# Attention, router and experts on one core: expert weights loaded in four parts, and row loads queued behind stores

## The chip, the cores and the metric

The kernel runs on one core of one Trainium2 chip. The metric is the device time of one launch in microseconds, the median of several runs without a profile. The profile is one further execution of the same program, and it is somewhat longer. A core has TensorE (PE in the profile; its weight loads are PEld), VectorE (DVE), ScalarE (ACT), GpSimd (POOL) and SyncE (SP). The last two also issue the DMA transfers here, and all transfers share 16 DMA engines.

## The reference

Block-causal attention with 8 batches, 8 heads, 576 positions and head size 64 gives 4608 rows of 512. A noisy router picks two of eight experts for each row, and an expert is two matrix products with a relu between them.

```python
scores = scale * np.matmul(q, k.transpose(0, 1, 3, 2))
mask = block_i >= block_j                    # blocks of 64 positions
attn = softmax(np.where(mask, scores, -1e9))
x = np.matmul(attn, v)                       # then as rows (4608, 512)
# ...
noisy_logits = x @ w_gate + np.log1p(np.exp(x @ w_noise)) * noise
top2 = np.argpartition(-noisy_logits, 2, axis=1)[:, :2]
top2_w = softmax of the two chosen logits
for e in range(8):                           # w1[e]: (512, 1024), w2[e]: (1024, 512)
    for k in range(2):
        mask = top2[:, k] == e
        h = np.maximum(x[mask] @ w1[e], 0.0)
        out[mask] += top2_w[mask, k, None] * (h @ w2[e])
```

## The kernel before

Attention goes through four groups of two batches, in 26 score slots each (`UG` = 26, `NG` = 4, so slots 0 to 103). A dictionary `at(slot, ...)` hangs other work on the slots: transposes, products with v, router steps, and scatters. A scatter writes 128 rows, sorted by expert, to an area `xd` in HBM; there are two halves of the rows, each with its own `xd` and `yd`.

The expert stage then works on 16 tiles. A tile is one expert and one half, 640 rows; the order is experts 0 to 3 of half 0, experts 0 to 3 of half 1, then experts 4 to 7 with both halves in turn. Layer 1 of a tile has 8 steps of 8 matmuls, layer 2 has 5 steps of 8. Step 0 of the next tile's layer 1 stands ahead of the layer 2 of this tile. Slots are counted on through these steps.

```python
def load_w(pool, e):                         # f32 in HBM, bf16 in SBUF: 1 MB each there
    w1sb = pool.tile([P, DB, F], BF16, tag="w1")
    nc.gpsimd.dma_start(out=w1sb, in_=moe_w1[e].rearrange("(b p) f -> p b f", p=P))
    w2sb = pool.tile([P, FB, Dm], BF16, tag="w2")
    nc.gpsimd.dma_start(out=w2sb, in_=moe_w2[e].rearrange("(b p) d -> p b d", p=P))
    wload[e] = (w1sb, w2sb)

def load_x(b):                               # rows of tile b, transposed on the way
    xg = ffn["x"].tile([P, DB, CAP], BF16, tag="xg", name="xg")      # 3 buffers
    ins = nc.sync.dma_start_transpose(out=xg, in_=xd[half][e * CAP:(e + 1) * CAP, 0:Dm])
    # ... waits for all scatters of the half

def layer1(b, fb):
    hp = sc_ps.tile([P, 2, 512], F32, tag="sc")                      # 2 buffers
    # ... 8 matmuls of 320 columns: hp <- w1sb, xg
    ins = nc.scalar.activation(out=hs[b][:, fb, :]..., in_=hp[:, :, 0:NW], func=AF.Relu)
    pace.append(ins.ins.name)

def layer2(b, c):
    yp = av_ps.tile([P, Dm], F32, tag="av")                          # 2 buffers
    # ... 8 matmuls of 512 columns: yp <- hs, w2sb
    if e + 1 < E:
        ysb = ffn["y"].tile([P, Dm], BF16, tag="ysb", bufs=4)
        nc.scalar.activation(out=ysb, in_=yp, func=AF.Copy, scale=w)
        nc.sync.dma_start(out=yd[half][...], in_=ysb)
    if c < LT[e]:                                                    # LT = 0,1,2,3,3,4,5,5
        yo = ffn["y"].tile([P, Dm], F32, tag="yo", bufs=4)
        nc.vector.scalar_tensor_tensor(out=yo, in0=yp, scalar=w, in1=ygs.pop((b, c)), ...)
        ins = nc.gpsimd.indirect_dma_start(out=out, ..., in_=yo)     # finished rows

def gather(b, c):                            # the rows' results of their other expert
    yg = ffn["y"].tile([P, Dm], BF16, tag="yg", bufs=GB, name="yg")  # 6 buffers
    ins = nc.gpsimd.indirect_dma_start(out=yg, ..., in_=yd[half][0:e * CAP, :], ...)
    tc.add_manual_dep(ins.ins, pace[-2], ...)

GJ = (2, 3, 4, 6, 7)                         # steps of layer 1 at which gathers go out
# ...
at(2 * UG + 24, load_w, wE, 0)
at(3 * UG + 15, load_w, wE, 1)
for u in range(NG * UG):
    score_unit(*divmod(u, UG))
    run(u)
    if u == 3 * UG + 18:
        # ... pools for rows and for expert 2
        load_x(0); load_rec(0); load_x(1); load_x(2); load_w(wM, 2)
# ...
for fn, b, j in steps:
    fn(b, j)
    if fn is layer1:
        if j == 0 and b and b + 2 < NB and b + 2 != 4:
            load_x(b + 2)
        if (b, j) == (3, 4):
            load_rec(1)
            load_x(4)
        if (b, j) in WL:
            load_w(*WL[b, j])
        if j in GJ and GJ.index(j) < LT[SEQ[b][1]]:
            gather(b, GJ.index(j))
    run(slot)
    slot += 1
    if slot == NG * UG + 6:
        # ... pools
        load_w(wL, 3)
        WL = {(5, 7): (wE, 4), (7, 3): (wE, 5), (9, 3): (wM, 6), (11, 3): (wL, 7)}
```

Every engine takes its instructions in the order of the program. A scatter or a gather waits for a recent activation (`pace[-2]`), which spreads these over time. Weights have no such wait; they wait for their buffers alone.

Of the kernel before, what the change touches and what calls it, by code (L numbers as in the profile page):

```python
# [9 lines left out]
BF16 = mybir.dt.bfloat16  # L10
# [9 lines left out]
def kernel(  # L20
# [12 lines left out]
    nc = tc.nc  # L33

    B, H, S, D = q.shape
    N, Dm = out.shape
    E = moe_w_gate.shape[1]
    F = moe_w1.shape[2]
    assert Dm == H * D and N == B * S
    P = 128  # L40
    DB = Dm // P
    FB = F // P
# [21 lines left out]
    UG = 2 * UN  # L64
# [32 lines left out]
    wE = main.enter_context(tc.tile_pool(name="wE", bufs=2))  # L97
# [109 lines left out]

    wload = {}

    def load_w(pool, e):  # L210
        w1sb = pool.tile([P, DB, F], BF16, tag="w1")
        nc.gpsimd.dma_start(out=w1sb, in_=moe_w1[e].rearrange("(b p) f -> p b f", p=P))
        w2sb = pool.tile([P, FB, Dm], BF16, tag="w2")
        nc.gpsimd.dma_start(out=w2sb, in_=moe_w2[e].rearrange("(b p) d -> p b d", p=P))
        wload[e] = (w1sb, w2sb)


    def transpose_qk(g, nm, ch):
# [256 lines left out]
    def load_x(b):  # L475
        half, e = SEQ[b]
        xg = ffn["x"].tile([P, DB, CAP], BF16, tag="xg", name="xg")
        ins = nc.sync.dma_start_transpose(out=xg, in_=xd[half][e * CAP:(e + 1) * CAP, 0:Dm])
        for nm in scat[half]:
            tc.add_manual_dep(ins.ins, nm, SYNC_DEP, reason="rows landed")  # L480
        xgs[b] = xg

    def load_rec(half):
        rc = rec_pool.tile([P, E, CT, NREC], I32, tag="rc", name="rc")
        ins = nc.sync.dma_start(out=rc.rearrange("p e c w -> p (e c) w"),
                                in_=xd[half].bitcast(I32)[0:OVB, Dm // 2:Dm // 2 + NREC]
                                .rearrange("(c p) w -> p c w", p=P))
        for nm in scat[half]:
            tc.add_manual_dep(ins.ins, nm, SYNC_DEP, reason="rows landed")
        rs[("rc", half)] = rc  # L490
# [76 lines left out]
    def gather(b, c):  # L567

        half, e = SEQ[b]
        yg = ffn["y"].tile([P, Dm], BF16, tag="yg", bufs=GB, name="yg")  # L570
        if len(gathers) < GB:
            nc.gpsimd.memset(yg, 0.0)
        gathers.append(b)
        ins = nc.gpsimd.indirect_dma_start(  # L574
            out=yg, out_offset=None, in_=yd[half][0:e * CAP, :],
            in_offset=bass.IndirectOffsetOnAxis(ap=orows[half][:, e, c:c + 1], axis=0),
            bounds_check=e * CAP - 1, oob_is_err=False)
        tc.add_manual_dep(ins.ins, pace[-2], SYNC_DEP, reason="spreads the descriptors over time")
        ygs[(b, c)] = yg
# [8 lines left out]
    NB = len(SEQ)  # L588
# [3 lines left out]
    def at(slot, fn, *args):  # L592
        todo.setdefault(slot, []).append((fn, args))

    def run(slot):
        for fn, args in todo.pop(slot, ()):
            fn(*args)
# [96 lines left out]
            at(r0 + r1 + j, scatter, g, j)  # L694
    at(8, clear_x, 0, 7)
    at(UG + 8, clear_x, 1, UG + 7)
    at(2 * UG + 24, load_w, wE, 0)
    at(3 * UG + 15, load_w, wE, 1)
    for u in range(NG * UG):
        score_unit(*divmod(u, UG))  # L700
        run(u)
        if u == 3 * UG + 18:
            raws_up.close()
            ffn["x"] = raws_up.enter_context(tc.tile_pool(name="xgp", bufs=3, side="right", reuse_waits="tile"))
            wM = raws_up.enter_context(tc.tile_pool(name="wM", bufs=1, side="right", reuse_waits="tile"))
            load_x(0)
            load_rec(0)
            load_x(1)
            load_x(2)
            load_w(wM, 2)  # L710

    slot = NG * UG
    at(slot + 6, read_rec, 0)
# [8 lines left out]
    for i in range(2):  # L722
        run(slot)
        slot += 1
    WL = {}
    for fn, b, j in steps:
        fn(b, j)
        if fn is layer1:
            if j == 0 and b and b + 2 < NB and b + 2 != 4:
                load_x(b + 2)  # L730
            if (b, j) == (3, 4):
                load_rec(1)
                load_x(4)
            if (b, j) == (4, 3):
                read_rec(1)
# [7 lines that stand above are left out]
            top.close()  # L743
            wL = top.enter_context(tc.tile_pool(name="wL", bufs=1, reuse_waits="tile"))
            ffn["y"] = top.enter_context(tc.tile_pool(name="yp", bufs=4, reuse_waits="tile"))
            load_w(wL, 3)
            WL = {(5, 7): (wE, 4), (7, 3): (wE, 5), (9, 3): (wM, 6), (11, 3): (wL, 7)}
    assert not todo, sorted(todo)
    sched.__exit__(None, None, None)

# [5 lines left out]
    with tc.If(rs["over"] > 0):  # L756
# [4 lines left out]
        for g in range(NG):  # L761
# [5 lines left out]
            for idx in range(TG):  # L767
                for p0, tok in token_blocks(g, idx):
                    nc.sync.dma_start(out=token_order(tok_w[tok:tok + 64, :]), in_=wd[p0:p0 + 64, g, idx, :])
                    nc.sync.dma_start(out=token_order(tok_s[tok:tok + 64, :]),  # L770
                                      in_=slots[p0:p0 + 64, g * TG + idx, 0:1])
        for half in range(NH):
            with tc.For_i(half * TH * P, (half + 1) * TH * P, P) as r0:
# [6 lines left out]
                    out=xo.bitcast(I32), out_offset=None, in_=xd[half].bitcast(I32),  # L780
# [9 lines left out]
                for e in range(E):  # L790
                    load_w(fb_w, e)
                    w1sb, w2sb = wload[e]
# [44 lines left out]
```

The softmax here doesn't subtract the row's maximum and nothing guards it: scores larger than these inputs give would overflow.

## Time and profile before

| | |
|---|---|
| Time, median of 3 runs | 541.73 us (540.43 to 545.04) |
| Span of the profiled execution | 564.4 us |
| Mean granted TensorE clock | 0.856 |
| DMA | 79.76 MB moved, 141 GB/s mean; 101365 of 140949 packets under 512 B |
| Weight loads | 16 of 1 MB, issued by GpSimd, 0.84 us (w1) and 0.96 us (w2) of GpSimd each |
| Transposing row loads | 16, issued by SyncE, 2.3 to 18.2 us of SyncE each, median 5.2 |
| Scatters, gathers, stores of finished rows | 72, 46 and 46, about 1 us of GpSimd each |

The page gives the busy time of each engine and its share of the span, then the span in 40 slices of 14.1 us: a digit is the busy share of a slice in tenths, and PEclk is the clock that TensorE was granted, in tenths of full speed. A row of the groups has the line of the kernel, engine, operation, what is written and read, the shapes and the count, then the busy time and the mean length of one, then the idle time just before them and who ended it. A timeline has start and length in us; the brackets hold the idle time before it and its releaser. Instructions of the same kind that follow each other are one row with a count. In the chain of waits each row is a piece of the chain that ended last: start, length, what it was. A GpSimd row that issues a DMA shows the time of issuing alone; where the chain names a DMA, the row runs from its issue to its landing.

### The profile page before, as it was taken

Reading aid. Unit: us, or ns where it says so; the run is one execution under the profiler, and the core shown is the slowest. Engines: PE = TensorE matmul, PEld = TensorE weight load, DVE = VectorE, ACT = ScalarE, POOL = GpSimd, SP = SyncE. Lnnn points to the kernel's source line nnn. Section 1 sums busy time; section 2 is a strip of 40 time slices with the busy share of each in tenths; the row PEclk is TensorE's granted clock in tenths of the full one; section 3 lists DMA queues with packets and bytes.
Section 4 is the critical chain, followed back from the end, with each engine's and each line's share of the span. In section 5 each row is a group of like instructions: output and inputs, shape, how many; then the busy total and the mean of one; then the engine's idle time right before and its main releaser. Section 6 shows DMA issues by size and latency. Waiting matters only on the chain.

```text
span 564.4 us, 9944 instructions
## 1 busy us (share of the span) xinstructions
PE 446.0 (79%) x3944; PEld 268.1 (48%) x3944; DVE 175.5 (31%) x490; ACT 238.9 (42%) x319; POOL 247.2 (44%) x291
## 2 busy tenths in 40 slices
PE   3796976796778668786969996977986995999980
PEld 2464654464345445444535553543553562555540
DVE  4474795388348627200103000100100201112220
ACT  1856754454446313333425442442451451554210
POOL 9683454583744416375322021142242452556550
PEclk9857976778676569998979997997997997999995
DMA  9999998295946999832582496496597588634230
GB/s 137 135 166 229 96 212 175 80 102 99 154 143 120 188 204 195 205 130 84 148 123 80 94 157 123 120 156 154 156 157 175 146 159 210 136 120 146 104 105 27
DMA packets 140949, 79.76 MB, mean 141 GB/s; under 512 B 101365, under 2 KB 130807, under 8 KB 140896
## 3 DMA queue, kind: packets, MB, share of 16 engines
q0 software_dynamic: 70304, 55.78, 59.6%
q1 hardware_dynamic: 70592, 23.27, 20.4%
q8 instruction: 33, 0.54, 0.4%
q14 instruction: 20, 0.16, 0.1%
HBM read 68.28 MB, written 34.21 MB: 182 GB/s over the span
## 4 chain that ended last, share of the span: by engine, by line
PE 46%; DMA 17%; issue 14%; POOL 9%; DVE 7%; ACT 3%; another core or an unknown queue 1%; POOLq 0%; SPq 0%; DVEq 0%; ACTq 0%
PE hp L533 16%; PE yp L545 15%; DMA xg<-xd 6%; PE sc L276 4%; POOL yg L574 4%; POOL out_dram L556 3%; PE av L313 3%; PE tp L238 2%; DMA yg<-yd,orow 2%; PE av L324 2%; DMA t<-in_q_dram 2%; PE tp L342 2%; DMA t<-in_k_dram 2%; DMA vt<-in_v_dram 2%; DMA out_dram<-yo,trow 1%
## 5 line engine op out<-in xcount | busy, mean ns | idle before, releaser
L533 PE MATMUL hp<-xg,w1sb 128*128 128x320 bf16 x1024 | 150.8, 308 | 26.6 <-ACT hq L536 15.0
L545 PE MATMUL yp<-w2sb,hq 128*128 128x512 bf16 x640 | 150.5, 393 | 25.5 <-DVE yo L554 21.5
L533 PEld LDWEIGHTS <-w1sb 128*128 128x128 bf16 x1024 | 102.6, 101 | 72.5 <-issue 23.2
L279 ACT ACTIVATE esc<-sc 128x1024 bf16<-128x1024 f32 x96 | 95.1, 1028 | 85.6 <-PE sc L276 53.9
L536 ACT ACTIVATE hq<-hp 128x640 bf16<-128x640 f32 x128 | 89.6, 704 | 88.7 <-PE hp L533 81.1
L554 DVE SCALAR_TENSOR_TENSOR yo<-yp,wrow,yg 128x512 f32<-128x512 f32 x46 | 34.3, 750 | 283.5 <-ACT ysb L550 200.1
L545 PEld LDWEIGHTS <-hq 128*128 128x128 bf16 x640 | 64.0, 100 | 106.6 <-issue 37.9
L459 POOL DMA_INDIRECT xd<-xr,slots x72 | 71.6, 995 | 79.6 <-issue 34.4
L550 ACT ACTIVATE ysb<-yp,wrow 128x512 bf16<-128x512 f32 x70 | 48.1, 687 | 121.4 <-PE yp L545 97.7
L556 POOL DMA_INDIRECT out_dram<-yo,trow x46 | 45.8, 996 | 110.7 <-DVE yo L554 107.3
L574 POOL DMA_INDIRECT yg<-yd,orow x46 | 47.2, 1027 | 81.9 <-ACT hq L536 54.5
L276 PE MATMUL sc<-hq 64*128 64x512 bf16 (+4 forms) x320 | 48.4, 372 | 11.5 <-ACT esc L279 9.9
L313 PE MATMUL av<-vt,esc 128*128 128x65 bf16 x640 | 38.8, 221 | 7.8 <-DVE xr L328 6.1
L313 PEld LDWEIGHTS <-esc 128*128 128x128 bf16 x640 | 30.5, 114 | 23.7 <-DVE xr L328 10.6
L205 POOL DMA_DIRECT2D vt<-in_v_dram x40 | 33.8, 876 | 14.7 <-PE av L324 10.6
L238 PE MATMUL tp<-ident,t 128*64 128x128 bf16 x512 | 29.4, 285 | 7.2 <-DVE hq L243 3.9
L328 DVE TENSOR_TENSOR xr<-av,rden 128x256 bf16<-128x256 f32 x72 | 30.6, 424 | 2.5
L238 PEld LDWEIGHTS <-t 128*64 128x64 bf16 x512 | 23.3, 149 | 15.8 <-DMA t<-in_q_dram 7.2
L245 DVE COPY hq<-tp 128x1024 bf16<-128x1024 bf16 (+1 forms) x24 | 25.0, 1042 | 6.3 <-PE tp L238 3.7
L327 DVE RECIPROCAL rden<-av 128x4 f32<-128x4 f32 x72 | 12.6, 174 | 43.6 <-PE av L313 15.2
L324 PE MATMUL av<-vt,esc 128*64 128x65 bf16 (+1 forms) x320 | 17.2, 226 | 10.9 <-issue 6.3
L276 PEld LDWEIGHTS <-hq 64*128 64x128 bf16 x320 | 12.5, 100 | 21.7 <-issue 14.4
(118 smaller groups left out, 213.8 us busy)
## 6 DMA issues: line engine op xcount, KB each, us to landing
yd<-ysb SPq DMA_DIRECT2D x70, 128.0 KB
w1sb<-in_moe_w_dram POOLq DMA_DIRECT2D x8, 1024.0 KB
w2sb<-in_moe_w_dram POOLq DMA_DIRECT2D x8, 1024.0 KB
t<-in_q_dram POOLq DMA_DIRECT2D x16, 256.0 KB
t<-in_k_dram POOLq DMA_DIRECT2D x16, 256.0 KB
vt<-in_v_dram POOLq DMA_DIRECT2D x32, 128.0 KB
xd<-zero SPq DMA_DIRECT2D x32, 99.0 KB
nz_all<-in_moe_noise_dram SPq DMA_DIRECT2D x72, 2.0 KB
```

What stands on the lines that cost most here:

```text
L238: nc.tensor.transpose(to[64 * hf:64 * hf + 64, :, r, :], raw[:, hf, r * 64:(r + 1) * 64], ident)
L276: nc.tensor.matmul(out=sc[:, hf, off:off + z - a], lhsT=kT[sl, c0 + jt * P:c0 + jt * P + P], rhs=qT[sl, c0 + a:c0 + z], start=True, stop=True)
L279: ins = nc.scalar.activation(out=esc[:, hh, :, piece * 512:(piece + 1) * 512], in_=sc, func=AF.Exp, scale=scale)
L313: nc.tensor.matmul(out=av[:, hh, :], lhsT=esc[:, hh, hf, c:c + P], rhs=vb[:, 4 * hf + jt, h, :], start=(jt == 0), stop=(jt == ib))
L459: ins = nc.gpsimd.indirect_dma_start(out=xd[half].bitcast(I32), out_offset=bass.IndirectOffsetOnAxis(ap=slots[:, g * TG + idx, i:i + 1], a ...
L533: nc.tensor.matmul(out=hp[:, n, 0:NW], lhsT=w1sb[:, db, fb * P:(fb + 1) * P], rhs=xgs[b][:, db, n * NW:(n + 1) * NW], start=(db == 0), sto ...
L536: ins = nc.scalar.activation(out=hs[b][:, fb, :].rearrange("p (n w) -> p n w", n=2), in_=hp[:, :, 0:NW], func=AF.Relu)
L545: nc.tensor.matmul(out=yp, lhsT=hs[b][:, fb, c * P:(c + 1) * P], rhs=w2sb[:, fb, :], start=(fb == 0), stop=(fb == FB - 1))
L550: nc.scalar.activation(out=ysb, in_=yp, func=AF.Copy, scale=w)
L554: nc.vector.scalar_tensor_tensor(out=yo, in0=yp, scalar=w, in1=ygs.pop((b, c)), op0=ALU.mult, op1=ALU.add)
L556: ins = nc.gpsimd.indirect_dma_start(out=out, out_offset=bass.IndirectOffsetOnAxis(ap=trow[half][:, e, c:c + 1], axis=0), in_=yo, in_offse ...
L574: ins = nc.gpsimd.indirect_dma_start(out=yg, out_offset=None, in_=yd[half][0:e * CAP, :], in_offset=bass.IndirectOffsetOnAxis(ap=orows[hal ...
```

## The change

Each expert's weights go out in four transfers in place of two: two halves of w1, then two halves of w2. For experts 0 to 3 the four parts hang on slots of the attention stage or of the first expert steps. For experts 4 to 7 they go to steps 1 and 5 of two consecutive tiles. The load of a tile's rows moves from step 0 of layer 1 to step 1, and since the layer 2 of the tile before stands between these two steps, the load comes behind that layer's stores in SyncE's queue. The purpose is to keep the transfers of weights from holding up other transfers, and the row loads from holding up the stores.

```diff
-    def load_w(pool, e):
-        w1sb = pool.tile([P, DB, F], BF16, tag="w1")
-        nc.gpsimd.dma_start(out=w1sb, in_=moe_w1[e].rearrange("(b p) f -> p b f", p=P))
-        w2sb = pool.tile([P, FB, Dm], BF16, tag="w2")
-        nc.gpsimd.dma_start(out=w2sb, in_=moe_w2[e].rearrange("(b p) d -> p b d", p=P))
-        wload[e] = (w1sb, w2sb)
+    def load_w(pool, e, k=None):
+        if not k:
+            wload[e] = (pool.tile([P, DB, F], BF16, tag="w1", name="w1sb"),
+                        pool.tile([P, FB, Dm], BF16, tag="w2", name="w2sb"))
+        for t, src in zip(wload[e], (moe_w1[e], moe_w2[e])):
+            n = t.shape[1]
+            w = src.rearrange("(b p) c -> p b c", p=P)
+            if k is None:
+                nc.gpsimd.dma_start(out=t, in_=w)
+            elif (k < 2) == (n == DB):
+                b0 = (k % 2) * n // 2
+                nc.gpsimd.dma_start(out=t[:, b0:b0 + n // 2], in_=w[:, b0:b0 + n // 2])
# ...
-    at(2 * UG + 24, load_w, wE, 0)
-    at(3 * UG + 15, load_w, wE, 1)
+    for k in range(4):
+        at(2 * UG + (14, 18, 22, 26)[k], load_w, wE, 0, k)
+        at(3 * UG + (2, 6, 10, 13)[k], load_w, wE, 1, k)
# ... at slot 3 * UG + 18
-            load_w(wM, 2)
+            for k in range(4):
+                at(u + (1, 3, 5, 7)[k], load_w, wM, 2, k)
# ... in the expert stage
-            if j == 0 and b and b + 2 < NB and b + 2 != 4:
+            if j == 1 and b and b + 2 < NB and b + 2 != 4:
                 load_x(b + 2)
# ... at slot NG * UG + 6
-            load_w(wL, 3)
-            WL = {(5, 7): (wE, 4), (7, 3): (wE, 5), (9, 3): (wM, 6), (11, 3): (wL, 7)}
+            for k in range(4):
+                at(slot + 3 * k + 1, load_w, wL, 3, k)
+            for i, pool in enumerate((wE, wE, wM, wL)):
+                for k in range(4):
+                    WL[5 + 2 * i + k // 2, (1, 5)[k % 2]] = (pool, 4 + i, k)
```

## The prediction

> **What bounds the kernel now.** I read the page first for the two stages, then the timeline of TensorE for its gaps, then the chain of waits and the queues' timelines inside one gap.
>
> ```profile
> PE 446.0 (79%) x3944; PEld 268.1 (48%) x3944; DVE 175.5 (31%) x490; ACT 238.9 (42%) x319; POOL 247.2 (44%) x291
> PEclk9857976778676569998979997997997997999995
> DMA  9999998295946999832582496496597588634230
> L533 PE MATMUL hp<-xg,w1sb 128*128 128x320 bf16 x1024 | 150.8, 308 | 26.6 <-ACT hq L536 15.0 <-DMA xg<-xd 11.5
> L545 PE MATMUL yp<-w2sb,hq 128*128 128x512 bf16 x640 | 150.5, 393 | 25.5 <-DVE yo L554 21.5 <-ACT ysb L550 2.4 <-ACT hq L536 1.5
> ```
>
> TensorE leads, but 79% is an average. The attention stage ends near 195 us; from there TensorE runs sixteen tiles of 640 rows, 64 matmuls of layer 1 and 40 of layer 2 each. From about 300 us on the DMA row shows peaks every 43 us or so, each followed by a fall of the clock row: the weight loads. The two matmul rows name what stood before them: rows not there (xg), or an eviction that came late (L536, L554). The timeline of TensorE has the gaps themselves (start, length, and in brackets the idle time and its releaser):
>
> ```profile
> 202.22 2.29 PE L533 MATMUL hp<-xg,w1sb 128*128 128x320 bf16 x8 [7.02 <-DMA xg<-xd]
> 236.67 6.68 PE L533 MATMUL hp<-xg,w1sb 128*128 128x320 bf16 x48 [3.32 <-ACT hq L536]
> ...
> 261.81 8.35 PE L533 MATMUL hp<-xg,w1sb 128*128 128x320 bf16 x48 [5.02 <-ACT hq L536]
> ...
> 290.94 2.31 PE L533 MATMUL hp<-xg,w1sb 128*128 128x320 bf16 x8 [4.49 <-DMA xg<-xd]
> ...
> 345.50 9.26 PE L533 MATMUL hp<-xg,w1sb 128*128 128x320 bf16 x48 [5.15 <-ACT hq L536]
> ...
> 384.94 5.28 PE L545 MATMUL yp<-w2sb,hq 128*128 128x512 bf16 x16 [7.58 <-DVE yo L554]
> ...
> 428.66 5.59 PE L545 MATMUL yp<-w2sb,hq 128*128 128x512 bf16 x16 [7.11 <-DVE yo L554]
> ...
> 472.36 5.93 PE L545 MATMUL yp<-w2sb,hq 128*128 128x512 bf16 x16 [6.77 <-DVE yo L554]
> ```
>
> The last four repeat once per weight load of experts 4 to 7, which GpSimd issues at 325.32, 367.91, 410.78 and 454.82 us. Between them TensorE has no gap worth naming: 64 matmuls of layer 1 take 8.69 us and 40 of layer 2 take 8.69 us on the chain of waits. Now inside the gap that ends at 384.94: first GpSimd's timeline, then SyncE's, then the chain.
>
> ```profile
> 367.91 0.85 POOL L212 DMA_DIRECT2D w1sb<-in_moe_w_dram  x1
> 369.27 0.92 POOL L214 DMA_DIRECT2D w2sb<-in_moe_w_dram  x1 [0.51 <-PE hp L533]
> 370.49 1.09 POOL L574 DMA_INDIRECT yg<-yd,orow  x1 [0.30 <-issue]
> ```
>
> ```profile
> 353.70 2.52 SPq L478 DMA_TRANSPOSE xg<-xd  x1
> ...
> 371.07 10.67 SPq L478 DMA_TRANSPOSE xg<-xd  x1
> 381.84 9.50 SPq L551 DMA_DIRECT2D yd<-ysb  x5
> ```
>
> ```profile
> 370.49 13.55 DMA yg<-yd,orow
> ...
> 384.94 5.28 PE yp L545 x16
> ```
>
> Two mechanisms work at once. (a) A gather of 128 rows is queued right behind 2 MB of weights and lands 13.55 us after its issue; VectorE's combine waits for it, and the two layer-2 buffers fill. (b) A transposing load of rows takes SyncE 2.52 us[...] and 10.67 us beside the weights; the five stores of the layer-2 tile stand behind it in the same queue. In the gap that ends at 345.50 it is (b) that counts: the transposing load holds SyncE from 328.44 to 338.62, and ScalarE waits 6.9 us for a store of `ysb` to give its buffer back. The start of the expert stage is (a) for xg: its first transposing load, issued at 176.21 amid two experts' weights (174.59 to 177.99), lands after 25.96 us by the chain.
>
> **What the Trainium skill says.** DMA: Bandwidth & Descriptors, "Queues, rings and completion order": a queue's descriptors are consumed in order, and an engine with work in several queues takes turns. The trace agrees: the gather waits for the weights ahead of it, and by the packet records the first xg (2560 packets of 256 bytes) gets 472 to 713 of them per 5 us while weights flow, against 2560 in some 6 us near 272 us with little else there. TensorE: Matmul & The Clock Gate, "HAM oscillation — how this bites in real kernels": idle gaps of about 3.4 us halve the matmul clock until TensorE has been busy again. The trace agrees: over 382 to 387 us the granted clock is 0.50, and the 16 matmuls after the gap take 5.28 us where 16 × 8.69 / 40 = 3.48 would do. The same DMA page, "Rules for kernel authors", speaks against splitting: transfers of 1 MB or more. Here a load is 1 MB and its halves 0.5 MB; no run yet shows their price, but already the full loads flow as 2048- and 1024-byte packets, which halving a tile along its blocks does not shorten.
>
> **The change, part by part.**
>
> Removed: bursts. From the packet records w1 flows at about 463 packets of 2048 bytes per 5 us, w2 at some 780 of 1024 bytes per 5 us. So w1 takes 512 × 5 / 463 = 5.5 us, w2 1024 × 5 / 780 = 6.6 us, one expert 12 us, and a quarter about 3 us. The bytes stay.
>
> Experts 4 to 7: parts go to steps 1 and 5 of two consecutive tiles, some 4.3 us apart in layer 1 and then a layer 2 away. A gather then has at most one quarter ahead of it, 3 us in place of 12. Gather c of the part at step 5 goes out in step 6 or 7 and is first needed after 1.1 + 1.1 + 4 × 1.74 = 9 us: hidden. The last part arrives a tile and a half before use for expert 4 (it goes out at step 5 of tile 6 for tile 8), longer than its 3 us by ten times. Four gaps: 5.15 + 7.58 + 7.11 + 6.77 = 26.6 us. The slow restarts after them: 5.28, 5.59 and 5.93 against 3.48 give 1.8 + 2.1 + 2.4, and 48 layer-1 matmuls in 9.26 against 48 × 8.69 / 64 = 6.52 give 2.7; sum 9.1. Together 35.7 us. I take 90% of it, **32 us**.
>
> First rows: expert 1 moves from slot 93 to slots 80 to 91, under the scores, where the DMA row falls to 4 and 6. Expert 2's first two parts have no pacing between them, so 1 MB still meets the first xg, not 4 MB. I expect it to land by about 186 us, before the scores end at 195. Gain 7.02 plus the slow first two groups (2.29 and 1.84 against 1.09 each): **9 us**.
>
> 231 to 262 us: the 3.32 us gap comes from stores that SyncE issues only at 229.85, after 38.48 us of transposing loads; it should go. The gaps of 2.42 and 5.02 are less clear: there the stores land promptly, and TensorE's own completions come late while scatters flow. I keep half of them: gain 3.3 + 3.7 = **7 us**.
>
> Row loads behind the stores: from tile 4 on, the load still goes out some 24 us before use, so nothing is lost and mechanism (b) falls away. But at tile 3 it costs. Before, the load for tile 5 went out at 272.24, ahead of the stores; then the records at 280.06 and the load for tile 4 at 280.53, landing at 290.9, late by 4.49. Now tile 5's 5 to 6 us stand between the stores and tile 4's load on the same queue. I expect that gap to grow to about 8 us: **loss 4 us**.
>
> GpSimd: 16 more issues. A half of w1 has 256 rows like a `t` load (0.72 us), a half of w2 has 512 like a full w1 (0.85): 3.1 in place of 1.8 us per expert, 11 us in all, on an engine 44% busy; scatters and the earlier loads beside q, k and v get **1 us** of loss.
>
> Scores of ScalarE, its 96 exponentials at 1028 ns, and the tail from 550.92 to 564.4 stay as they are. Sum: 32 + 9 + 7 − 4 − 1 = 43 us of the profiled span. The times without a profile lie 23 us below that span (541.73 against 564.4), and some of the gaps may be smaller there, so I scale by 0.83: 36 us, and 541.73 − 36 = 506.
>
> **Rivals.** (1) DMA becomes the bound. A pair of tiles late on moves about 7.4 MB (410 to 455 us: 159 to 171 GB/s over 45 us); in 35 us that is 212 GB/s. Five-microsecond windows reach 263 and 287 GB/s, so it should fit, but not by much; if it doesn't, half of the 36 us comes back: 521 to 525. (2) The load at 0.5 MB and the late load for tile 4 cost more than reckoned, or GpSimd's queue, busy with scatters until 270 us, holds the parts and gathers: some 515. (3) Transfers were hidden anyway: against it stand the four gaps tied to four loads; it would leave 540. (4) All gaps but tile 4's go, with their restarts: 51 us of the span, and 490 to 495.
>
> **Range and chances.** Rival 4 sets the low end and rival 1 the high end: 493 to 522. To miss 2% the gain would have to be under 10.8 us, less than a third of the sum of the four late gaps. Faster by over 2%: 0.93; within 2%: 0.05; slower: 0.02.
>
> **What would show it.** In the profile after, TensorE's timeline should have no gap over 2 us from 300 us on; the gathers should land within about 6 us; the transposing loads should hold SyncE 2.5 to 5 us; the first xg should land before the scores end; the DMA row should be level, not peaked; the gap ahead of tile 4 should be larger than 4.49 us. I am wrong if the gaps come back in other places under a DMA row at 9, or if tile 4's gap passes 12 us.

## The result and the profile after

The changed kernel takes 510.31 us (median of 4 runs, 508.31 to 512.66) against 541.08 us for the kernel before on the same chip: ratio 0.9421, 95% interval 0.935 to 0.9492. The prediction said 506, with 493 to 522 as its range.

One fact has to stand ahead of every comparison. The kernel before takes some 541 us on some chips and some 565 us on others. Its profile must have come from a chip of the second kind (that execution took 566.5 us, and base_again below shows that a profile by itself does not lengthen a run); the profile after comes from one of the first. So the two profiles differ by more than the change, and the experiments below are compared with the kernel before on their own chip. Single executions of the changed kernels also scatter by 2 to 3%, so the ratios of the experiments leave out the profiled execution and disturbed ones, and those of x4_first and split_again rest on two executions.

The page of the kernel after, the rows that answer to those shown of before:

```profile
PE 427.9 (84%) x3944; PEld 260.3 (51%) x3944; DVE 174.3 (34%) x490; ACT 239.5 (47%) x319; POOL 257.9 (50%) x307
...
PEclk9869787786597559999979999999999979899995
DMA  8999999689999998983564459889999999954330
...
L540 PE MATMUL hp<-xg,w1sb 128*128 128x320 bf16 x1024 | 145.8, 303 | 17.5 <-DMA xg<-xd 17.5
L552 PE MATMUL yp<-w2sb,hq 128*128 128x512 bf16 x640 | 147.9, 389 | 11.0 <-DVE yo L561 11.0
```

The peaks of the DMA row have run together: for eleven slices, from 306 to 447 us, it stands at 8 or 9. The eviction (ACT hq) is gone from the idle time ahead of both matmul groups, and the combine's share there has halved, 21.5 to 11.0. The wait for rows is larger. (The DMA row adds up the times of the packets, as a share of the engines' time. The sum can pass 1: it was 1.32 in the kernel before at 339 to 344 us.) TensorE's timeline has the gaps of the expert stage (all over 1 us):

```profile
184.42 2.29 PE L540 MATMUL hp<-xg,w1sb 128*128 128x320 bf16 x8 [11.73 <-DMA xg<-xd]
...
246.47 3.61 PE L552 MATMUL yp<-w2sb,hq 128*128 128x512 bf16 x16 [1.38 <-DVE yo L561]
...
263.46 2.32 PE L540 MATMUL hp<-xg,w1sb 128*128 128x320 bf16 x8 [5.77 <-DMA xg<-xd]
...
359.04 5.39 PE L552 MATMUL yp<-w2sb,hq 128*128 128x512 bf16 x24 [1.64 <-DVE yo L561]
...
413.92 2.56 PE L552 MATMUL yp<-w2sb,hq 128*128 128x512 bf16 x8 [2.43 <-DVE yo L561]
...
418.62 5.17 PE L552 MATMUL yp<-w2sb,hq 128*128 128x512 bf16 x16 [2.15 <-DVE yo L561]
...
438.15 7.03 PE L552 MATMUL yp<-w2sb,hq 128*128 128x512 bf16 x24 [2.21 <-DVE yo L561]
```

The four late gaps of 5.15 to 7.58 us have become four of 1.6 to 2.4. The first gap has not gone, and tile 4's has grown. SyncE's timeline, two row loads and the stores of one tile:

```profile
276.98 2.48 SPq L485 DMA_TRANSPOSE xg<-xd  x1
...
339.06 7.32 SPq L558 DMA_DIRECT2D yd<-ysb  x5
346.47 5.17 SPq L485 DMA_TRANSPOSE xg<-xd  x1
```

A row load beside weights holds SyncE 5.17 us in place of 10.67 (4.40 to 7.41 from 311 to 425 us), and the five stores ahead of it go out at the pace of the tile.

### The profile page after: what moved, and what is told of

It is laid out like the page before. It is cut to its first block, busy times and chain, and to the rows that moved or that the text cites. A ratio compares the mean times of both kernels' runs of the same rounds, so it can differ in the third digit from the quotient of the medians.

```text
span 510.8 us, 9962 instructions
## 1 busy us (share of the span) xinstructions
PE 427.9 (84%) x3944; PEld 260.3 (51%) x3944; DVE 174.3 (34%) x490; ACT 239.5 (47%) x319; POOL 257.9 (50%) x307
## 4 chain that ended last, share of the span: by engine, by line
PE 36%; DMA 23%; issue 12%; DVE 11%; POOL 11%; ACT 3%; SPq 2%; POOLq 0%; DVEq 0%; ACTq 0%
PE yp L552 14%; PE hp L540 13%; DMA yg<-yd,orow 9%; DMA xg<-xd 5%; DMA t<-in_q_dram 4%; POOL out_dram L563 3%; POOL yg L581 3%; ACT esc L286 2%; PE sc L283 2%; DMA vt<-in_v_dram 2%; PE tp L245 2%; DVE xr L335 2%; SPq L620 2%; PE av L331 2%; PE av L320 1%
## 5 line engine op out<-in xcount | busy, mean ns | idle before, releaser
L540 PE MATMUL hp<-xg,w1sb 128*128 128x320 bf16 x1024 | 145.8, 303 | 17.5 <-DMA xg<-xd 17.5
L552 PE MATMUL yp<-w2sb,hq 128*128 128x512 bf16 x640 | 147.9, 389 | 11.0 <-DVE yo L561 11.0
L540 PEld LDWEIGHTS <-w1sb 128*128 128x128 bf16 x1024 | 100.9, 99 | 60.1 <-issue 11.8
L581 POOL DMA_INDIRECT yg<-yd,orow x46 | 46.9, 1019 | 55.7 <-ACT hq L543 46.3
L283 PE MATMUL sc<-hq 64*128 64x512 bf16 (+4 forms) x320 | 46.6, 361 | 8.0 <-ACT esc L286 6.4
L320 PE MATMUL av<-vt,esc 128*128 128x65 bf16 x640 | 36.4, 214 | 4.0 <-DVE xr L335 3.5
L245 PE MATMUL tp<-ident,t 128*64 128x128 bf16 x512 | 29.4, 285 | 10.3 <-DMA t<-in_q_dram 5.3
L320 PEld LDWEIGHTS <-esc 128*128 128x128 bf16 x640 | 28.4, 110 | 17.7 <-DVE xr L335 7.8
L335 DVE TENSOR_TENSOR xr<-av,rden 128x256 bf16<-128x256 f32 x72 | 30.6, 424 | 2.5
L252 DVE COPY hq<-tp 128x1024 bf16<-128x1024 bf16 (+1 forms) x24 | 25.0, 1042 | 4.7 <-PE tp L245 4.3
L250 DVE COPY hq<-tp 128x1024 bf16<-128x1024 bf16 (+1 forms) x24 | 14.9, 622 | 21.6 <-PE tp L245 21.0
L283 PEld LDWEIGHTS <-hq 64*128 64x128 bf16 x320 | 12.1, 100 | 18.2 <-issue 10.7
```

The costliest lines, as they stand in the source:

```text
L245: nc.tensor.transpose(to[64 * hf:64 * hf + 64, :, r, :], raw[:, hf, r * 64:(r + 1) * 64], ident)
L283: nc.tensor.matmul(out=sc[:, hf, off:off + z - a], lhsT=kT[sl, c0 + jt * P:c0 + jt * P + P], rhs=qT[sl, c0 + a:c0 + z], start=True, stop=True)
L320: nc.tensor.matmul(out=av[:, hh, :], lhsT=esc[:, hh, hf, c:c + P], rhs=vb[:, 4 * hf + jt, h, :], start=(jt == 0), stop=(jt == ib))
L335: nc.vector.tensor_tensor(out=xr[:, idx, st * SET * D:(st + 1) * SET * D].rearrange("p (h d) -> p h d", h=SET), in0=av[:, :, 0:D], in1=rde ...
L540: nc.tensor.matmul(out=hp[:, n, 0:NW], lhsT=w1sb[:, db, fb * P:(fb + 1) * P], rhs=xgs[b][:, db, n * NW:(n + 1) * NW], start=(db == 0), sto ...
L552: nc.tensor.matmul(out=yp, lhsT=hs[b][:, fb, c * P:(c + 1) * P], rhs=w2sb[:, fb, :], start=(fb == 0), stop=(fb == FB - 1))
```

## The experiments

Changes of the median against the kernel before on the same chip, and from each profile the gaps of TensorE (first rows; tile 4; the sum of the late gaps over 1 us, from 300 us to the last tile). The last column is the time from tile 5 to tile 15, which is where experts 4 to 7 are loaded, taken between the first layer-1 evictions of ScalarE in the two tiles. It was 212.5 us in the profile of before and 186.8 in the profile after, and ten tiles without any wait would take 10 × (8.69 + 8.69) = 173.8. A median covers all executions of a run, the profile is one of them.

| run | before, us | this, us | change | ratio, 95% interval | first rows | tile 4 | late | tiles 5 to 15 |
|---|---|---|---|---|---|---|---|---|
| base_again | 565.83 | 566.82 | | one run | 8.68 | 3.84 | 26.5 | 212.7 |
| order_only | 565.83 | 555.49 | −10.3 | 0.9811, 0.9732 to 0.989 | 7.55 | 5.89 | 19.4 | 204.2 |
| parts_at_once | 565.83 | 552.87 | −13.0 | 0.9765, 0.97 to 0.9829 | 7.62 | 5.89 | 18.4 | 203.2 |
| split_only | 565.83 | 534.39 | −31.4 | none given, runs too scattered | none | 4.24 | 2.9 | 181.0 |
| late_only | 540.31 | 518.87 | −21.4 | 0.9558, 0.9492 to 0.9624 | 15.64 | 6.58 | 16.1 | 198.0 |
| after_again | 540.31 | 509.75 | −30.6 | 0.9449, 0.9364 to 0.9533 | 1.71 | 6.14 | 3.0 | 178.2 |
| split_again | 540.31 | 506.24 | −34.1 | 0.9307, 0.9233 to 0.938 | 1.07 | 3.72 | 2.8 | 177.6 |
| x4_first | 540.31 | 499.75 | −40.6 | 0.9101, 0.9023 to 0.9179 | 16.85 | none | 8.9 | 186.8 |
| no_late_weights | 565.02 | 518.15 | −46.9 | 0.9195, 0.9138 to 0.9253 | none | 6.29 | none | 176.8 |
| early_later | 565.02 | 523.90 | −41.1 | 0.9294, 0.9228 to 0.936 | none | none | 8.9 | 192.0 |
| late_earlier | 565.02 | 523.29 | −41.7 | 0.9265, 0.9185 to 0.9345 | none | none | 10.0 | 189.7 |
| early_later_2 | 543.12 | 510.84 | −32.3 | 0.9361, 0.9285 to 0.9436 | none | none | 13.7 | 196.1 |

**base_again**, the kernel before once more.

> The kernel before, unchanged, profiled once more. Its first profile had a span of 564.4 us against 541 us without a profile, the scores ending at 195 us, and completions of TensorE that came up to 6 us late around 250 us. If those 23 us belong to that one execution, this span is 540 to 546, the scores end between 172 and 180 us, the gaps of 2.42 and 5.02 us near 250 to 262 us are gone or under 1 us, and the gaps at the weight loads of experts 4 to 7 are still 5 to 8 us. If they belong to the kernel, the span is again about 564.

Span 564.8, median of before on that chip 565.83. The scores end near 195 us again and the late gaps are the same within 0.6 us. The 23 us belong to the chip, not to the profile. What is slower there shows best in one kernel that ran on both kinds of chip (early_later and early_later_2): the first half of its attention keeps step (an exponential at 93.38 and at 93.81 us), then the slower chip falls back, and the last score matmul starts at 188.14 and 174.65. The scatters start near 89 us.

**order_only**: the row load at step 1, weights whole at the old places.

```diff
-            if j == 0 and b and b + 2 < NB and b + 2 != 4:
+            if j == 1 and b and b + 2 < NB and b + 2 != 4:
```

> The kernel before with one part alone: row loads at step 1, behind the stores; weights whole, at the old places. My theory: the gap of expert 4 (stores behind the row load) goes, the three gaps of experts 5 to 7 (gathers behind 2 MB of weights) stay near 7 us, tile 4's gap grows by 3 to 5 us: 534 to 543 us. Rival, that the order does most: 510 to 520.

It gains 10.3 us where I expected up to 7 (the interval stays below 1, but a gain of 2% is not certain). Its profile shows the theory's picture, though: expert 4's gap, which came from stores behind a row load, is gone, and the three gaps of gathers behind weights stay.

```profile
290.91 2.31 PE L533 MATMUL hp<-xg,w1sb 128*128 128x320 bf16 x8 [5.89 <-DMA xg<-xd]
...
375.98 5.34 PE L545 MATMUL yp<-w2sb,hq 128*128 128x512 bf16 x16 [7.52 <-DVE yo L554]
...
418.57 6.22 PE L545 MATMUL yp<-w2sb,hq 128*128 128x512 bf16 x16 [5.92 <-DVE yo L554]
...
462.62 6.38 PE L545 MATMUL yp<-w2sb,hq 128*128 128x512 bf16 x16 [5.93 <-DVE yo L554]
```

The late gaps lose 26.5 − 19.4 = 7.1 us, and tiles 5 to 15 as a whole 212.7 − 204.2 = 8.5, most of the 10.

**parts_at_once**: four parts and the new order, but all four parts of an expert in one go.

```diff
-                load_w(*WL[b, j])
+                for k in range(4):
+                    load_w(*WL[b, j], k)          # at the old places; experts 0 to 3 alike
```

> Four parts for each expert and the new order of row loads, but all four parts of an expert go out at once at the old places. My theory: what counts is the spread, not the size; 2 MB still stand ahead of the gathers, so within 4 us of the run with the order alone: 534 to 545. Rival, that half-size transfers by themselves free the queues: 508 to 520.

2.6 us below the order alone, and the intervals overlap. The three gaps of experts 5 to 7 are still there:

```profile
372.18 5.75 PE L552 MATMUL yp<-w2sb,hq 128*128 128x512 bf16 x16 [7.18 <-DVE yo L561]
...
415.09 6.47 PE L552 MATMUL yp<-w2sb,hq 128*128 128x512 bf16 x16 [5.83 <-DVE yo L561]
...
458.88 5.07 PE L552 MATMUL yp<-w2sb,hq 128*128 128x512 bf16 x16 [5.40 <-DVE yo L561]
```

Halving the transfers neither costs nor frees anything that these runs can show; what counts is when they go out. The Trainium skill (DMA: Bandwidth & Descriptors, "Rules for kernel authors") gives 1 MiB or more per DMA as the way to the most bandwidth; here 0.5 MB cost nothing that can be measured, and by the packet records the packets stay at 2048 and 1024 bytes.

**split_only and split_again**: the spread without the order.

```diff
-            if j == 1 and b and b + 2 < NB and b + 2 != 4:
+            if j == 0 and b and b + 2 < NB and b + 2 != 4:
```

> The changed kernel with one part undone: the row load goes out at step 0 again, ahead of the stores; the weights stay in spread parts. My theory: the spread of the weights does most. A transposing load beside one quarter holds SyncE some 5 us in place of 10, which the four store buffers mostly absorb, and tile 4's rows go out earlier, so 508 to 517 us, ratio to before 0.94 to 0.955. Rival, that the order of loads and stores does most: 530 us or more. Rival, that the order of the changed kernel costs more at tile 4 than it gains: 500 to 507.

> The changed kernel with the row load back at step 0, ahead of the stores, a second time, now beside the changed kernel. The first runs scattered from 522 to 537 us, and its profile shows gaps of 10.2 and 8.3 us near 230 and 258 us with the stores standing behind three row loads. Theory: the order is worth those gaps at the start of the expert stage and nothing later: 5 to 15 us slower than the changed kernel on the same chip. Rival, that the order is neutral once the weights are spread: within 4 us of it.

The first took 534.39 us against 565.83, with single runs from 521.76 to 537.04; that is too scattered for a verdict, though 534.39 / 565.83 = 0.944 lies within the 0.94 to 0.955 that I expected. The second took 506.24 next to 509.75 for the changed kernel, single runs 503.0 to 511.6 and 499.5 to 516.6. So once the weights are spread, the order brings nothing that can be measured here. The rival, no difference, fits best, but my theory is not refuted: the two profiled executions took 506.82 without the order and 499.47 with it. In the profile the start is worse without the order, tile 4 better:

```profile
213.45 8.64 PE L540 MATMUL hp<-xg,w1sb 128*128 128x320 bf16 x48 [5.07 <-ACT hq L543]
...
255.16 7.19 PE L540 MATMUL hp<-xg,w1sb 128*128 128x320 bf16 x40 [2.87 <-ACT hq L543]
...
266.07 2.32 PE L540 MATMUL hp<-xg,w1sb 128*128 128x320 bf16 x8 [3.72 <-DMA xg<-xd]
```

From tile 5 on the order seems to be worth nothing at all. Without it the ten tiles take 181.0 and 177.6 us, near the 176.8 with no late weights; in the six with the order and the same spread of late weights they take 178.2 to 198.0. Whether a load behind the stores costs something there was not tested by itself.

**after_again and late_only**: the changed kernel again, and with experts 0 to 3 loaded whole.

```diff
-    for k in range(4):
-        at(2 * UG + (14, 18, 22, 26)[k], load_w, wE, 0, k)
-        at(3 * UG + (2, 6, 10, 13)[k], load_w, wE, 1, k)
+    at(2 * UG + 24, load_w, wE, 0)
+    at(3 * UG + 15, load_w, wE, 1)                # experts 2 and 3 alike
```

> The changed kernel, unchanged, beside the kernel before on one chip and next to the three runs below. The first comparison gave a ratio of 0.942 where the kernel before takes 541 us; the runs so far were on a chip where it takes 566. Expected here: ratio 0.93 to 0.95 whatever the level of the chip. If the chip's slower attention stage hides the first row load, the gap of 11.7 us ahead of layer 1 is under 3 us here.

> The changed kernel with experts 0 to 3 loaded whole at the old places; only experts 4 to 7 are spread, and row loads stand behind the stores. Theory: the late gaps and their restarts are about 30 us, of which the order alone got one; so between the order alone (ratio 0.981) and the changed kernel (0.942), nearer to the latter: ratio 0.945 to 0.96. Rival, that most of the gain comes from the early loads under the scores: ratio above 0.965.

On one chip: −30.6 us for the whole, −21.4 without the early part. The early spread is then worth about 9 us, the late one with the order about 21; the intervals of the two ratios overlap. Where the 9 us arise is not shown. In late_only the first rows come 15.64 us late, beside the weights of two experts, but with the early weights spread that gap was 1.71 us here, 11.73 in the first profile and 16.85 in x4_first: it varies from one execution to the next. The rest of late_only's profile loses most in tiles 5 to 15 (198.0 against 178.2 us), where its code is that of the changed kernel. That a slow chip's attention hides the first row load could not be seen on this fast chip. split_only and no_late_weights show it, with the same early code on chips at 565: neither has a gap there. The spread is needed for it, as order_only and parts_at_once, also at 565, wait 7.55 and 7.62 us.

**x4_first**: the rows of tile 4 ahead of the records and tile 5's rows.

```diff
-            if j == 1 and b and b + 2 < NB and b + 2 != 4:
+            if j == 1 and b and b + 2 < NB and b + 2 not in (4, 5):
                 load_x(b + 2)
-            if (b, j) == (3, 4):
-                load_rec(1)
+            if (b, j) == (3, 1):
                 load_x(4)
+                load_rec(1)
+                load_x(5)
```

> The changed kernel with the rows of tile 4 asked for first after the stores of tile 2 (step 1 of tile 3), then the records, then the rows of tile 5. In the changed kernel TensorE waits 5.77 us for tile 4's rows, which stand behind tile 5's and the records, and restarts slowly (some 2.5 us more). Theory: this wait goes wholly: 6 to 8 us less than the changed kernel on the same chip. Rival, that the wait moves to the records, which the gathers and stores of tile 4 need: 0 to 2 us less.

The median is 10 us below the changed kernel's on the same chip (expected 6 to 8). Single executions, 491.3 to 508.2 against 499.5 to 516.6, overlap, so the size is uncertain; the gap at tile 4 is gone and did not come back at the records. It has the lowest median and ratio of the kernels that do the whole work. SyncE's queue in its profile: tile 4's rows first, then the records, then tile 5's.

```profile
254.63 2.78 SPq L485 DMA_TRANSPOSE xg<-xd  x1
257.51 0.52 SPq L492 DMA_DIRECT2D rc<-xd  x1
258.13 6.85 SPq L485 DMA_TRANSPOSE xg<-xd  x1
```

**no_late_weights**: the loads of experts 4 to 7 left out; these experts compute with the weights of experts 0 to 3.

```diff
             if (b, j) in WL:
-                load_w(*WL[b, j])
+                pool, e, k = WL[b, j]
+                wload[e] = wload[e - 4]
```

> The changed kernel with the weights of experts 4 to 7 left out: these experts compute with the tiles of experts 0 to 3, so the output is not the reference's and 8 MB of transfers fall away. It tells what the spread weights still cost. Theory: the waits for combines from 350 to 440 us (8.4 us in the profile after) come from DMA engines near their limit, and go when the weights go: 8 to 15 us less than the changed kernel, ratio to before 0.915 to 0.93, no such wait over 0.5 us in its profile from 300 us on. Rival, that they come from the gathers and result stores themselves: waits of the same size stay, ratio 0.94 to 0.945.

No wait for a combine over 0.5 us is left from 300 us on, so the late waits do come from the weights. The run takes away both the part that stands ahead of a gather and the traffic beside it, so it can't tell these two apart. One tile's length in each profile, first the kernel after, then this one (stretch, length, busy us and count of TensorE, its weight loads, VectorE, ScalarE and GpSimd, clock, DMA share, GB/s):

```profile
357.00:374.00 17.00, 15.36 (x95) 9.19 (x94) 2.25 (x3) 8.39 (x12) 7.62 (x8) 1.00 1.05 203
374.00:391.00 17.00, 17.00 (x103) 9.97 (x102) 2.25 (x3) 8.71 (x13) 8.76 (x9) 1.00 1.02 202
```

```profile
377.00:394.00 17.00, 17.00 (x103) 9.97 (x102) 2.25 (x3) 8.89 (x13) 5.86 (x6) 1.00 0.48 136
394.00:411.00 17.00, 17.00 (x104) 9.96 (x103) 1.89 (x3) 9.06 (x13) 7.05 (x7) 1.00 0.51 150
```

With spread weights the packets' times add up to the whole of the DMA engines' time, without them to half. It ran on a chip at 565 us, where the changed kernel was not timed; against early_later there (which has no gap at tile 4, while this one has 6.29) it is 5.8 us faster. So the spread weights still cost some 6 us, and with tile 4's gap set right about 12. This is a rough estimate from the two runs, since their early loads differ too.

**early_later, early_later_2 and late_earlier**: with tile 4's rows first, experts 1 to 3 later; then also experts 4 to 7 earlier.

```diff
-        at(3 * UG + (2, 6, 10, 13)[k], load_w, wE, 1, k)
+        at(3 * UG + (2, 6, 23, 25)[k], load_w, wE, 1, k)
-                at(u + (1, 3, 5, 7)[k], load_w, wM, 2, k)
+                at(u + (9, 12, 15, 18)[k], load_w, wM, 2, k)
-                at(slot + 3 * k + 1, load_w, wL, 3, k)
+                at(slot + 3 * k + 7, load_w, wL, 3, k)
```

```diff
+            when = [(5, 1), (5, 5), (6, 1), (6, 5), (6, 7), (7, 1), (7, 5), (7, 7),
+                    (8, 1), (8, 5), (8, 7), (9, 1), (9, 5), (9, 7), (10, 1), (10, 5)]
```

> The changed kernel with tile 4's rows first (as in the run before) and with less ahead of the first row load: the second half of expert 1's weights goes out 13 to 15 slots later, expert 2's 8 to 11 slots later, expert 3's 6 later. Theory: the first row load waited until 164 to 168 us for scatters that stand behind weights, and then shared the engines with expert 2; now it is issued near 160 us and lands before the scores end, so the first gap (1.7 to 16.9 us in the profiles) is under 1 us: ratio to before 0.895 to 0.91, and less scatter of the times. Rival, that the weights then collide with the stores and gathers of tiles 0 to 2: the gap goes and comes back there, 0.91 to 0.925.

> The kernel with tile 4's rows first and the weights of experts 1 to 3 later, a second time. Its first run was on a chip whose attention stage is slow enough to hide the first row load in any kernel, so its main point is untested. On a chip where the kernel before takes 541 us: the first row load is issued some 5 us earlier than in the changed kernel (near 161 us), beside fewer weights, and the gap ahead of layer 1 is under 1 us; 492 to 500 us. Rival, that the row load is slow by itself beside the scatters of the second half: a gap of 2 to 17 us stays and the time is that of the run with tile 4's rows first, 491 to 508. On a chip at 565 us it would repeat 521 to 527.

> As the run before, and the parts of experts 4 to 7 go out in tiles 5 to 10 in place of 5 to 12, three parts for a tile, because the later tiles have more gathers and result stores. Theory: the waits for combines after 340 us (2 to 8 us) go: 3 to 8 us less than the run before. Rival, that the denser parts only move the waits to tiles 6 to 9: within 2 us of it, either way.

The first row load behaves as planned. In early_later_2, on a chip at 543 us, SyncE's timeline has it 3.7 us earlier than in the profile after and without a hold-up, and the gap ahead of layer 1 is gone:

```profile
162.75 2.61 SPq L485 DMA_TRANSPOSE xg<-xd  x1
```

The time does not follow: 510.84, not 492 to 500. Its late gaps sum to 13.7 us in place of 8.9 in x4_first, though the late part is the same code, and its scores ended some 9 us later than there. The runs don't tell whether the shifted weights cause this. early_later itself missed its 0.895 to 0.91, and 0.9294 is above its rival's range too. late_earlier came within 0.6 us of early_later: denser parts only move the waits, as the rival said.

## Why the prediction was right, point by point

**The four late gaps (expected 32 of 35.7 us).** The mechanism holds: parts_at_once keeps the gaps, the spread takes them away. The size depends on the execution. In the first profile gaps of 26.6 us became 8.4; the restarts, 9.1 us before, are now 5.39 − 5.21, 2.56 − 1.74, 5.17 − 3.48 and 7.03 − 5.21, sum 4.5. So 22.8 us were won, too few. In after_again, the same kernel, only two gaps are left:

```profile
409.27 3.61 PE L552 MATMUL yp<-w2sb,hq 128*128 128x512 bf16 x16 [1.73 <-DVE yo L561]
...
426.33 5.39 PE L552 MATMUL yp<-w2sb,hq 128*128 128x512 bf16 x24 [1.31 <-DVE yo L561]
```

Their 3.0 us and 0.3 us of slow restarts make 32.4 us won, which is the forecast. One quarter stands ahead of a gather, as said (GpSimd issues one at 400.38 and the gather at 402.84). What failed in both executions is the "3 us in place of 12" behind it, and with it the 6 us for a gather. In the chain of the kernel after a gather still takes 10.70 and 14.79 us, in that of after_again 9.19 and 9.39. The prediction has 9 us until a gather is first needed, so a gather near 9 us costs little and one of 14 us doesn't hide:

```profile
347.35 10.70 DMA yg<-yd,orow
...
402.84 14.79 DMA yg<-yd,orow
```

I had counted the quarter ahead, not the row loads, result stores and tile stores that share the engines when nothing is idle any more. That this is the reason is argued, not shown: a DMA share of 0.93 to 1.07 in every tile from 340 to 447 us, and no such wait without the weights, fit it. It would be rival 1 in part. The clock also differs from the 3.4 us that the prediction cites: after gaps of 2.43 and 2.21 us here it fell to 0.50, over 415 to 421.8 and 439 to 442 us, and the matmuls after them ran slowly; after 1.73 and 1.31 us in after_again it stayed at 1.00.

**First rows (expected 9).** On the kind of chip that it was read from, this holds: in no_late_weights, with the same early code, the load is issued at 176.38, its last packet ends at 183.7, and layer 1 starts without a gap. (One reading was off: near 272 us the 2560 packets took some 3 us, not 6.) On the fast chip it does not hold. There the load is issued at 166.42 and lands after 17.96 us on the chain, but the scores end near 173, and the wait is 11.73 (1.71 in after_again). The early spread as a whole pays about 9 us (late_only against after_again).

**231 to 262 us (expected 7).** Gaps of 10.8 us became 2.6 (0.80 + 0.40 + 1.38), but the chips differ. On the fast chip the gaps without the order are 5.07 + 2.87 us there (split_again), while SyncE spends 25.03 us on three row loads and ScalarE waits 11.6 us for stores, so the reason given, stores behind row loads, is shown. The amount is not: on a chip at 565, no_late_weights with the new order and spread early weights has gaps of 1.26, 5.95 and 4.03 us at 232 to 252, as much as before.

**Tile 4 (expected gap 8, loss 4).** The gap is 5.77 and 6.14 us against 4.49 and 3.84: a loss of 1.3 to 2.3. The sign was right, and x4_first shows that the place in the queue is its cause.

**GpSimd.** Expected 11 us more, measured 257.9 − 247.2 = 10.7.

**The other signs.** The DMA row is level, as said. Gaps over 2 us from 300 us on should have gone: three of 2.15 to 2.43 stand in the first profile, none in after_again. SyncE should be held 2.5 to 5 us by a row load; from tile 4 on it is 2.42 to 7.41.

**The scale of 0.83.** Its reason, that a profile makes gaps larger, is wrong: base_again takes as long without one. The 43 us were read on a chip at 565 and the gain was measured at 541, where it is 30.8. The changed kernel was not timed at 565. The only kernel timed on both, early_later, gained 41.1 us at 565 and 32.3 at 543, so a gain read off the slower chip does seem to shrink on the faster one, by about as much as the discount took off. That 506 came so near to 510.31 is thus partly luck: a discount with a wrong cause, beside a term for the first rows that fails on the fast chip and one for 231 to 262 us that fails on the slower.

## What to carry to other kernels

A large load in front of small urgent transfers cost here what the whole burst takes, so cut it and give each part a place of its own in time; cutting alone did nothing. Reordering the queue gained about 10 us while the burst was there, and nothing that could be measured once it was spread. Then look at what the levelled traffic adds up to: with a DMA share near 1, denser parts only moved the waits (late_earlier). A single dependent transfer at a phase change (tile 4's rows here) may be worth a third of the whole change, and its cure is its place in the queue. And repeat the profile before you size a term by it: six profiles with the same late code and the same order have late gaps from 3.0 to 16.1 us.

## What was not expected of the hardware

The kernel before takes 541 us on some chips and 565 on others. In early_later, timed on both, the scores end 13.5 us later on the slower one, of 13.1 us between the two medians, and the delay arises while scatters flow (from 89 us on). In the profile of before, from a slower chip, the last matmul of a group ends at 250.31 us by the timeline (such ends are modelled) and its eviction starts at 256.90, though the store before it had been issued at 252.70 and its packets were through. Why evictions come late there stays open.

The first row load ran at two speeds. By the packet records its 2560 packets of 256 bytes took 66.7 and 75.7 ns on average in the profiles after and x4_first, and 30.7 in after_again with the same code ahead of it; in the slow cases a tenth of them took 194 ns or more, and a tenth of the scatters' packets beside them over 0.8 us. The row load at 251 us of the profile after, with little beside it, took 18.2 ns a packet. What decides between the two was not found.
